# Two causal attentions, a low-rank MLP and a mixture of attention experts on one core: the first two attentions change how they sum, normalise and transpose their rows

## The chip, the cores and the metric

One core of a Trainium2 chip runs the whole program. The metric is the device time of one execution in microseconds (us); the median over several runs is compared. Besides the runs, one execution was taken with the hardware profiler; all durations below come from it.

## The reference

Batch B = 4, H = 12 heads, S = 448 positions, head size 64, model width D = 768, hidden width 3072, rank 32, 4 experts. Cut to what matters:

```python
scores = q @ k.T / 8                       # causal mask
attn = exp(scores - max); attn /= attn.sum(-1) + 1e-9
x = (attn @ v) as (B, S, 768)
h = x.T @ U @ V                            # U 448x32, V 32x448: along the positions
u = x + h.T
x = u + relu(u @ w_ch1) @ w_ch2            # 768 -> 3072 -> 768
...                                        # then top-2 of 4 single-head attention experts on x
```

The change lies in the first three lines of the attention and in the low-rank step, for batch elements 0 and 1.

## The kernel before, in words

Layout. Activations lie with the model width on the 128 partitions and the 448 positions along the free dimension; f32 data that TensorE multiplies in f16 is split into a high and a low half (`hi`, `lo`), and products are made of three passes (hi*hi, hi*lo, lo*hi; `PASS`). All of SBUF is one tensor, `arena`, all of PSUM one tensor, `bank`, of eight banks, so every row of the profile names only these two.

Attention of a batch element b (`attention`, L763) runs over six pairs of heads; pair n is 6 b + p. For each pair:

- `softmax` (L585): for each of two heads f32 score matmuls in four row blocks of 112 (widths 112, 224, 336, 448, because of the causal mask) into the score banks; VectorE adds the mask, finds the row extreme and writes the rows to SBUF (a custom reduction, printed as CUSTOM_DVE_ANT_0 by the profile and as ISA in the order of instructions); ScalarE takes the exponential of each block with the row sum as an accumulated output, then copies each block to f16 (`hi`); GpSimd subtracts to get `lo`; one DMA transpose per head brings hi and lo of the head's ten 112x112 blocks to the layout that the next matmul needs.
- `shares` (L641): from the row sums VectorE forms scaled reciprocals in 112x8 (add and scale, reciprocal, cast to f16, low half); 16 small matmuls spread them over the partitions, and ScalarE copies them to `y`.
- `weighted` (L662): 24 matmuls weight the values (three passes, four blocks, two heads that lie side by side in the array's columns), VectorE multiplies by `y`, ScalarE and GpSimd make f16 halves of the result (`XHL`).
- `lowrank` (L679): a DMA transpose of the halves (`XTR`), 12 f16 matmuls with the three-pass U (`U3`), ScalarE and VectorE bring the sum to f16 halves, one f16 matmul of 448 columns with V, and VectorE adds the result to x (the close of the pair). It is issued for pair n-1 while pair n is under way.

Meanwhile `weight_pair` (L819) decodes the f64 weights of the MLP, finds a power-of-two norm of each tile (four small VectorE steps on 128x2) and writes f16 halves; `mlp` (L898) multiplies. `ORDER` (L47) says which attention, MLP group and expert step follow which.

The order of the instructions. No call issues at once: `Program.add` (L195) records each operation with its engine, cost and key (its due time), and `Program.plan` (L241) makes one fixed list over all engines by keys that the table `SHIFTS` (L51) moves for each part of the program. Where the list leaves TensorE idle before `WARM_END` (210 us of the plan) or in the tail after the last attention, it inserts filler matmuls of zeros of 448 columns (`prog.idle`, L1334). These are instructions like others: on the chip TensorE runs them whether or not it would have had to wait. Every recorded operation has the line of the call in `issue` (L353), so rows are told apart by shape; only fillers have a line of their own.

Of the kernel before, what the change touches and what calls it, by code (L numbers as in the profile page):

```python
# [20 lines left out]
NP = H // 2  # L21
# [58 lines left out]
class Program:  # L80
# [6 lines left out]
    CHAIN = 0.0  # L87
    SLACK = 1.03
# [152 lines left out]
    def plan(self, keys, users):  # L241
# [15 lines left out]
        while len(order) < len(ops):  # L257
# [19 lines left out]
            o = ops[i]  # L277
            cost, fill = o["cost"] * self.SLACK, 0
# [78 lines left out]
def kernel(  # L357
# [96 lines left out]
    XHL = [view("xhl", i * 2048, 128, F16, 1024).rearrange("p (l s) -> p l s", l=2) for i in range(2)]  # L454
# [3 lines left out]
    U3 = view("u3", 0, 128, F16, 2 * NC * 3 * R).rearrange("p (l c r) -> p l c r", l=2, c=NC)  # L458
# [203 lines left out]
    def weighted(vs, pts, y, dst, coef=None, kind="o"):  # L662
        shares(y, coef)
        t = psum(kind)
        with prog.group():
            for i, (lp, lv_) in enumerate(PASS):
                for j in range(NC):
                    for h, (va, pt) in enumerate(zip(vs, pts)):
                        o = t[64 * h:64 * h + 64]
                        k0, kc, kj = LO_BLK if lp else HI_BLK  # L670
                        k = k0 + (kc + kj) * j
                        mm(o[:, C * j:S], va[:, j, 64 * lv_:64 * lv_ + 64],
                           pt[0:C, k:k + kc * (NC - 1 - j) + 1:kc],
                           i == 0 and j == 0, i == 2 and j == NC - 1)
        dve.tensor_tensor(out=y, in0=t[:, 0:S], in1=y, op=ALU.mult)
        act.activation(dst[:, 0, 0:S], y, AF.Copy)
        pool.tensor_tensor(out=dst[:, 1, 0:S], in0=y, in1=dst[:, 0, 0:S], op=ALU.subtract)

    def lowrank(n):  # L679
        b, p = divmod(n, NP)  # L680
        iv = IV[:, b:b + 1]
        tst = TST
        sp.dma_start_transpose(out=XTR, in_=XHL[n % 2].rearrange("p l s -> p (l s)"))
        t = psum("l")
        with prog.group():
            for c in range(NC):
                for i, (lu_, lx) in enumerate(PASS):
                    mm(t[0:96, 0:128], U3[:, lu_, c], XTR[:, 4 * lx + c], c == 0 and i == 0, c == NC - 1 and i == 2)
# [4 lines left out]
        mm(u[:, 0:S], tst, VST, True, True)  # L693
        dve.tensor_tensor_reduce(out=X3[b][:, p], in0=u[:, 0:S], in1=X3[b][:, p], scale=iv, scalar=BIG,
# [68 lines left out]
    def attention(b):  # L763
        if b == B - 1:
            prog.key = HT * 30
            zero_pads(SLOTS[b][1][2:])
        if not b:
# [3 lines left out]
        for p in range(NP):  # L771
# [6 lines left out]
            if p == NP - 1 and b + 1 < B:  # L778
                v_scale(b + 1)
            i = n % 2  # L780
            pts = [SLOTS[b][2][(2 * n + j) % len(SLOTS[b][2])] for j in range(2)]
            prog.key = HT * 2 * n
            softmax([[(QK[i][64 * j:64 * j + 64, 1], QK[i][64 * j:64 * j + 64, 0])] for j in range(2)], -0.125,
                    pts, slots=SLOTS[b][0:2])
            prog.key = HT * (2 * n + 1)
            weighted([VH[:, 2 * i + j] for j in range(2)], pts, X3[b][:, p], XHL[i])
# [32 lines left out]
    def weight_pair(i):  # L819
# [410 lines left out]
    UR = view("ring", 0, 128, I32, 2 * NC * R)  # L1230
    US = view("ring", 2048, 128, F32, NC * R)
    VR = view("ring", 4096, 96, I32, 2 * S)
    LV = view("ring", 8192, 96, F32, S)
# [14 lines left out]
    dve.memset(ONE, 1.0)  # L1248
    prog.key = 0.0
# [7 lines left out]
    for a in XHL:  # L1257
        dve.memset(a[:, :, S:512], 0.0)
# [4 lines left out]
    absmax(TMP[:, 5:6], US)  # L1263
# [16 lines left out]
    for r in range(3):  # L1280
        split(U3V[:, 0, :, r], U3V[:, 1, :, r], USV, SUV[:, 0:1])
# [99 lines left out]
```

## Time and profile before

| | us |
|---|---|
| runs (3): median, lowest, highest | 1050.6, 1049.38, 1054.52 |
| profiled execution: device time | 1048.72 |
| profiled execution: span in the trace | 1045.8 |
| TensorE busy (share of the span) | 1023.3 (98%) |
| VectorE busy | 698.5 (67%) |
| ScalarE busy | 617.8 (59%) |
| GpSimd busy | 466.8 (45%) |
| granted TensorE clock, mean | 0.998 |

The profile covers one execution. PE is TensorE, PEld its weight loads, DVE VectorE, ACT ScalarE, POOL GpSimd, SP the engine that issues all DMAs. Busy times of groups are unions of intervals; successive instructions overlap a little, so groups add up to somewhat more than the engine's total. Share of the span is an average over stages: the first 190 us hold attentions 0 and 1, then come MLP groups, experts and the other attentions.

### The profile page before, as it was taken

Reading aid. Unit: us, or ns where it says so; the run is one execution under the profiler, and the core shown is the slowest. Engines: PE = TensorE matmul, PEld = TensorE weight load, DVE = VectorE, ACT = ScalarE, POOL = GpSimd, SP = SyncE. Lnnn points to the kernel's source line nnn. Section 1 sums busy time; section 2 is a strip of 40 time slices with the busy share of each in tenths; the row PEclk is TensorE's granted clock in tenths of the full one; section 3 lists DMA queues with packets and bytes.
Section 4 is the critical chain, followed back from the end, with each engine's and each line's share of the span. In section 5 each row is a group of like instructions: output and inputs, shape, how many; then the busy total and the mean of one; then the engine's idle time right before and its main releaser. Section 6 shows DMA issues by size and latency. Waiting matters only on the chain.

```text
span 1045.8 us, 18647 instructions
## 1 busy us (share of the span) xinstructions
PE 1023.3 (98%) x6743; PEld 544.7 (52%) x6743; DVE 698.5 (67%) x1744; ACT 617.8 (59%) x1470; POOL 466.8 (45%) x500
## 2 busy tenths in 40 slices
PE   9999989999998999999999999999999999999998
PEld 4555545555544445644555644455555555655555
DVE  8989878878876677555657555588656577531364
ACT  6788987666754563568762569763552632622073
POOL 3576666433552440135540137567797891310011
PEclk9999999999999999999999999999999999999999
DMA  9999999467788786269994269983434345453023
GB/s 240 206 239 240 223 223 266 161 218 249 264 271 286 289 326 218 97 157 232 232 244 128 73 157 219 237 172 104 136 121 151 123 149 156 104 147 106 10 78 107
DMA packets 220139, 192.53 MB, mean 184 GB/s; under 512 B 176304, under 2 KB 179504, under 8 KB 220048
## 3 DMA queue, kind: packets, MB, share of 16 engines
q1 hardware_dynamic: 220048, 191.36, 67.1%
q8 instruction: 52, 0.85, 0.3%
q14 instruction: 39, 0.32, 0.1%
HBM read 112.16 MB, written 36.18 MB: 142 GB/s over the span
## 4 chain that ended last, share of the span: by engine, by line
PE 58%; DMA 6%; DVE 3%; ACT 2%; issue 1%; SPq 0%; DVEq 0%; ACTq 0%
PE bank L353 58%; DVE arena L353 3%; DMA arena<-arena 2%; DMA w<-arena 2%; ACT arena L353 1%; DMA arena<-in_w_dram 1%; PE bank L1334 1%; DMA arena<-in_v_dram 1%; DMA out_dram<-arena 1%; ACT bank L353 0%; SPq L353 0%; DVEq L353 0%; ACTq L353 0%
## 5 line engine op out<-in xcount | busy, mean ns | idle before, releaser
L353 PE MATMUL bank<-arena 128*128 128x448 f16 (+13 forms) x6341 | 945.5, 325 | 17.2 <-ACT arena L353 6.7
L353 POOL TENSOR_TENSOR arena<-arena 128x384 f16<-128x384 f32 (+8 forms) x493 | 465.8, 966 | 568.3 <-ACT arena L353 497.9
L353 PEld LDWEIGHTS <-arena 128*128 128x128 f16 (+5 forms) x5853 | 472.3, 104 | 411.2 <-issue 63.4
L353 ACT ACTIVATE arena<-arena 128x768 f16<-128x768 f32 (+12 forms) x872 | 479.9, 586 | 222.2 <-DVE arena L353 132.7
L353 DVE SCALAR_TENSOR_TENSOR arena<-arena 128x768 int32<-128x768 int32 (+7 forms) x193 | 179.2, 944 | 7.2 <-ACT arena L353 5.8
L353 DVE CUSTOM_DVE_ANT_0 arena<-bank,arena 112x224 f32<-112x224 f32 (+4 forms) x280 | 124.4, 476 | 58.6 <-PE bank L353 51.5
L353 DVE TENSOR_TENSOR arena<-bank,arena 128x448 f16<-128x448 f32 (+2 forms) x160 | 95.5, 599 | 101.4 <-ACT arena L353 75.7
L353 DVE SCALAR_TENSOR_TENSOR arena<-bank,arena 128x448 f32<-128x448 f32 (+1 forms) x138 | 84.6, 621 | 69.9 <-PE bank L353 59.4
L353 DVE TENSOR_SCALAR arena<-arena 128x1 f32<-128x1 f32 (+10 forms) x305 | 85.8, 308 | 46.5 <-ACT arena L353 19.4
L353 ACT ACTIVATE arena<-bank 128x448 f16<-128x448 f32 (+2 forms) x148 | 76.0, 518 | 47.7 <-PE bank L353 44.8
L353 DVE TENSOR_TENSOR arena<-arena 112x8 f16<-112x8 f32 (+10 forms) x136 | 82.4, 618 | 27.6 <-ACT arena L353 25.4
L353 ACT ACTIVATE bank<-bank,arena 128x448 f32<-128x448 f32 x72 | 43.0, 598 | 97.0 <-PE bank L353 96.8
L1334 PE MATMUL bank<-arena 128*128 128x448 f16 x402 | 88.5, 360 | 1.5 <-DVE arena L1251 1.0
L353 ACT ACTIVATE arena<-bank,arena 128x448 f32<-128x448 f32 (+2 forms) x73 | 33.0, 457 | 56.1 <-PE bank L353 53.3
L353 PEld LDWEIGHTS bank<-arena 64*112 64x112 f32 (+5 forms) x488 | 39.4, 169 | 43.1 <-issue 16.7
L353 DVE TENSOR_REDUCE arena<-arena 128x1 f32<-128x448 f32 (+8 forms) x107 | 57.7, 544 | 4.4 <-DMA arena<-in_v_dram 3.3
L1334 PEld LDWEIGHTS <-arena 128*128 128x128 f16 x402 | 37.4, 101 | 42.6 <-issue 12.2
L353 ACT ACTIVATION_READ_ACCUMULATOR arena<-arena 112x1 f32 (+1 forms) x304 | 57.3, 189 | 0.0
L353 DVE DVE_READ_ACCUMULATOR2_ANT arena<- 112x1 f32 (+1 forms) x280 | 22.8, 82 | 0.0
L353 DVE CAST arena<-arena 112x8 f16<-112x8 f32 x32 | 11.7, 372 | 1.7 <-PE bank L353 1.3
L353 DVE TENSOR_SCALAR arena<-bank 128x2 f32<-128x2 f32 x24 | 3.6, 152 | 6.1 <-PE bank L353 6.1
L353 DVE COPY arena<-bank 128x1 f32<-128x1 f32 (+2 forms) x14 | 2.2, 158 | 8.1 <-PE bank L353 8.1
(11 smaller groups left out, 18.8 us busy)
## 6 DMA issues: line engine op xcount, KB each, us to landing
arena<-w SPq DMA_DIRECT2D x138, 384.0 KB, 3.4
arena<-in_w_dram SPq DMA_DIRECT2D x48, 768.0 KB, 5.4
w<-arena SPq DMA_DIRECT2D x78, 384.0 KB, 4.9
arena<-in_qk_dram SPq DMA_DIRECT2D x24, 448.0 KB, 4.3
arena<-in_v_dram SPq DMA_DIRECT2D x24, 224.0 KB, 4.4
out_dram<-arena SPq DMA_DIRECT2D x24, 224.0 KB, 2.2
arena<-in_we_dram SPq DMA_DIRECT2D x6, 384.0 KB, 6.2
arena<-arena SPq DMA_TRANSPOSE x88, 4.9
```

The lines of the kernel that those rows point to most:

```text
L353: fn(*a, **k)
L1334: prog.idle = lambda late: nc.tensor.matmul(bank[:, 0 if late else 7, 64:512], ZERO.to_broadcast([128, 128]), ZERO.to_broadcast([128, S]), ...
```

## The change

For batch elements 0 and 1 `softmax`, `weighted` and `lowrank` are replaced; elements 2 and 3 and the experts keep the old functions.

- `packed`: the scores of both heads lie in one grid of 20 blocks of 112 columns. The exponentials have no accumulated sum. One ScalarE copy makes the f16 high half of all 20 blocks, four GpSimd subtractions of five blocks make the low half; one DMA transpose moves the high halves of both heads, another the low halves.
- `gathered`: row sums are made by 16 matmuls of the transposed halves with a block of ones (`ONE16`), two heads side by side, in the same loop as the 24 value matmuls. ScalarE copies the sums and adds epsilon, VectorE takes the reciprocal of 128x448 and multiplies. Four f32 matmuls with the identity transpose the result, ScalarE copies it out (`XNF`).
- `lowrank32`: four f32 matmuls with U (`UF`), a ScalarE copy, one f32 matmul of 448 columns with V, then the same closing step (`finish`). The DMA transpose of the f16 halves is gone for these pairs.
- `weight_pair`: three of the four norm steps work on the PSUM bank.
- The planner skips, when VectorE or GpSimd would wait more than 100 ns for the shared port, to an operation that needs none (`SKIP`); the table `SHIFTS` has new numbers throughout.

```diff
 SHIFTS = (
-    -77, -44428, 37506, -91735, 18953, 8775, 17019, -24054, -47040, 356689, 6182, -12585, -8654, 13276, -10536,
...
+    -43466, -27356, -10820, 4351, -7110, 8009, -7508, -69, -27832, 14181, 3461, 33477, -8645, -7372, 6786, -6709,
...
+    SKIP = 100.0
...
+            if o["port"] and port > t + self.SKIP:
+                held = []
+                while r and ops[r[0][1]]["port"] and len(held) < 64:
+                    held.append(heapq.heappop(r))
+                if r and len(held) < 64:
+                    j = heapq.heappop(r)[1]
+                    heapq.heappush(r, (keys[i], i))
+                    i, o = j, ops[j]
...
+    def packed(n):
...
+        for j in range(2):
+            for c in range(NC):
+                act.activation(rows(j, c), rows(j, c), AF.Exp, bias=mx[j][:, c:c + 1], scale=-1.0)
+        act.activation(hi[:, :, 0:C], grid, AF.Copy)
+        sp.dma_start_transpose(out=pts[0], in_=HALF[i][0])
+        for k in range(0, 20, 5):
+            pool.tensor_tensor(out=lo[:, k:k + 5, 0:C], in0=grid[:, k:k + 5], in1=hi[:, k:k + 5, 0:C],
+                               op=ALU.subtract)
+        sp.dma_start_transpose(out=pts[1], in_=HALF[i][1])
+        return pts
+
+    def gathered(n, pts):
...
+        den, num, t = psum("b"), psum("o"), psum("l")
+        for l, pt in enumerate(pts):
+            with prog.group():
+                for j in range(NC):
+                    for lv_ in ((None, 0, 1) if not l else (None, 0)):
+                        for h in range(2):
+                            va = ONE16 if lv_ is None else VH[:, 2 * (n % 2) + h, j, 64 * lv_:64 * lv_ + 64]
+                            o = (den if lv_ is None else num)[64 * h:64 * h + 64, C * j:S]
+                            k0, kc = (6 * j, 5) if h else (1 + 6 * j, 1)
+                            mm(o, va, pt[0:C, k0:k0 + kc * (NC - 1 - j) + 1:kc],
+                               not l and j == 0 and lv_ != 1, l == 1 and j == NC - 1)
+        act.activation(y, den[:, 0:S], AF.Identity, bias=EPSC)
+        dve.reciprocal(y, y)
+        dve.tensor_tensor(out=y, in0=num[:, 0:S], in1=y, op=ALU.mult)
+        with prog.group():
+            for c in range(NC):
+                mm(t[0:C, 128 * c:128 * c + 128], y[:, C * c:C * c + C], IDF, True, True)
+        act.activation(XNF[n % 2], t[0:C], AF.Copy)
+
+    def lowrank32(n):
+        b, p = divmod(n, NP)
+        t = psum("l")
+        with prog.group():
+            for c in range(NC):
+                mm(t[0:R, 0:128], UF[:, R * c:R * c + R], XNF[n % 2][:, 128 * c:128 * c + 128], c == 0, c == NC - 1)
+        act.activation(TSF[n % 2], t[0:R, 0:128], AF.Copy)
+        u = psum("l")
+        mm(u[:, 0:S], TSF[n % 2], LV[0:R], True, True)
+        finish(n, u)
...
-        dve.tensor_scalar(s, norm, FLOOR2, None, op0=ALU.max)
-        dve.tensor_scalar(bits(p), bits(s), 1, HALFM, op0=ALU.logical_shift_right, op1=ALU.bitwise_and)
-        dve.tensor_scalar(bits(s), bits(p), HALFM, None, op0=ALU.bitwise_xor)
-        dve.tensor_scalar(s, s, 2.0 ** 57, None, op0=ALU.mult)
+        dve.tensor_scalar(norm, norm, FLOOR2, None, op0=ALU.max)
+        dve.tensor_scalar(bits(p), bits(norm), 1, HALFM, op0=ALU.logical_shift_right, op1=ALU.bitwise_and)
+        dve.tensor_scalar(bits(norm), bits(p), HALFM, None, op0=ALU.bitwise_xor)
+        dve.tensor_scalar(s, norm, 2.0 ** 57, None, op0=ALU.mult)
```

How the instructions stand now. On VectorE, at the first pair's shares in the kernel before (the scale and the reciprocal of 112x8 lie between two score reductions; the cast and the low half follow some ten rows further on):

```order
L353 TENSOR_SCALAR arena<-arena 112x8
L353 ISA arena<-bank,arena 112x112
L353 ISA arena 112x1
L353 RECIPROCAL arena<-arena 112x8
L353 ISA arena<-bank,arena 112x336
L353 ISA arena 112x1
L353 COPY arena<-bank 128x2
L353 TENSOR_REDUCE arena<-bank 1x1
```

and on VectorE at the first pair's reciprocal in the changed kernel:

```order
L363 ISA arena<-bank,arena 112x4x112
L363 ISA arena 112x1
L363 RECIPROCAL arena<-arena 128x448
L363 ISA arena<-bank,arena 112x448
L363 ISA arena 112x1
L363 TENSOR_TENSOR arena<-bank,arena 128x448
L363 TENSOR_REDUCE arena<-arena 112x1 x2
L363 ISA arena<-bank,arena 112x112
```

The reciprocal is now of 448 elements and stands right ahead of a later pair's score reduction and of the product (TENSOR_TENSOR) that the transposes on TensorE need. On TensorE, at the start of the first low-rank group in the kernel before (12 matmuls of 96x128 that needed a DMA transpose; L1334 is the filler):

```order
L1334 LDWEIGHTS arena
L1334 MATMUL bank<-arena 128x448
L353 LDWEIGHTS arena
L353 MATMUL bank<-arena 96x128
L353 LDWEIGHTS arena
L353 MATMUL bank<-arena 96x128
```

and on TensorE at the first transposes of normalised rows in the changed kernel (L1447 is its filler, 112x128 the f32 transposes, 64x448 the next pair's row sums and values):

```order
L1447 LDWEIGHTS arena
L1447 MATMUL bank<-arena 128x448
L363 MATMUL bank<-arena 112x112 x2
L363 MATMUL bank<-arena 112x336 x2
L363 MATMUL bank<-arena 112x128 x4
L363 LDWEIGHTS arena
L363 MATMUL bank<-arena 64x448
```

What waited for a DMA transpose now waits for VectorE's product, with the next pair's row sums and values behind it in the list.

## Rows read from the trace of the kernel before

**Rows 1.** Head of the page: span; busy time, share and instructions of each engine.
```profile
span 1045.8 us, 18647 instructions
PE 1023.3 (98%) x6743; PEld 544.7 (52%) x6743; DVE 698.5 (67%) x1744; ACT 617.8 (59%) x1470; POOL 466.8 (45%) x500
```
**Rows 2.** Busy time by stage of the filler matmuls alone (L1334): PE, PEld.
```profile
0.00:200.00 200.00, 80.36 (x364) 33.78 (x364) 1.00 0.98 230
200.00:1000.00 800.00, 0.00 (x0) 0.00 (x0) 1.00 0.62 178
1000.00:1046.00 46.00, 8.12 (x38) 3.59 (x38) 0.99 0.34 89
```
**Rows 3.** Timeline of VectorE at the close of pair twelve: start, us, what.
```profile
189.10 0.68 DVE L353 CUSTOM_DVE_ANT_0 arena<-bank,arena 128x448 f32<-128x448 f32 x1
```
**Rows 4.** Busy time by stage, all engines; the first row names the columns.
```profile
core 0: us, PE busy (x) PEld busy (x) DVE busy (x) ACT busy (x) POOL busy (x), PEclk, DMA share, GB/s
0.00:190.00 190.00, 183.83 (x1407) 95.68 (x1408) 164.07 (x498) 150.56 (x409) 114.03 (x139) 1.00 1.00 230
```
**Rows 5.** Waits of VectorE, 0 to 190 us: total, times, longest.
```profile
DVE arena L353 <- PE bank L353: 15.9, 16, 3.4
DVE arena L353 <- ACT arena L353: 4.7, 8, 1.2
```
**Rows 6.** Timeline of TensorE, pieces of the first stage: fillers, shares, low rank, values, scores.
```profile
99.36 2.85 PE L1334 MATMUL bank<-arena 128*128 128x448 f16 x14
...
33.34 0.75 PE L353 MATMUL bank<-arena 112*64 112x112 f16 x16
...
109.98 0.83 PE L353 MATMUL bank<-arena 128*96 128x128 f16 x12
...
111.70 1.62 PE L353 MATMUL bank<-arena 112*64 112x448 f16 x24
...
107.30 1.01 PE L353 MATMUL bank<-arena 64*112 64x448 f32 x4
```
**Rows 7.** Groups by shape, weight loads: count, busy us, mean ns, idle before.
```profile
L353 PEld LDWEIGHTS bank<-arena 128*128 128x128 f32 x48 | 8.4, 194 | 11.2 <-ACT arena L353 10.0
```
**Rows 8.** Groups by shape, VectorE, 0 to 190 us.
```profile
L353 DVE CAST arena<-arena 112x8 f16<-112x8 f32 x12 | 7.5, 627 | 0.5 <-PE bank L353 0.5
L353 DVE TENSOR_SCALAR arena<-arena 128x2 int32<-128x2 int32 x13 | 6.5, 500 | 0.1
L353 DVE SCALAR_TENSOR_TENSOR arena<-bank,arena 32x128 f16<-32x128 f32 x12 | 4.1, 343 | 2.8 <-ACT arena L353 2.4
L353 DVE TENSOR_SCALAR arena<-arena 112x8 f32<-112x8 f32 x12 | 4.1, 339 | 1.4 <-ACT arena L353 1.3
L353 DVE TENSOR_TENSOR arena<-arena 112x8 f16<-112x8 f32 x12 | 3.4, 285 | 0.0
L353 DVE RECIPROCAL arena<-arena 112x8 f32<-112x8 f32 x12 | 2.3, 195 | 0.1
```
**Rows 9.** Groups by shape, VectorE: reciprocals from 430 us on, the others whole span.
```profile
L353 DVE RECIPROCAL arena<-arena 112x8 f32<-112x8 f32 x20 | 4.0, 202 | 0.6
L353 DVE RECIPROCAL arena<-arena 112x4 f32<-112x4 f32 x4 | 0.7, 178 | 0.1
...
L353 DVE TENSOR_REDUCE arena<-arena 128x1 f32<-128x448 f32 x48 | 29.3, 612 | 0.6
...
L353 DVE TENSOR_SCALAR arena<-bank 128x2 f32<-128x2 f32 x24 | 3.6, 152 | 6.1 <-PE bank L353 6.1
...
L353 DVE TENSOR_REDUCE arena<-arena 128x1 f32<-128x128 f32 x1 | 0.3, 275 | 0.0
```
**Rows 10.** Groups by shape, ScalarE and GpSimd, 0 to 190 us.
```profile
L353 ACT ACTIVATION_READ_ACCUMULATOR arena<-arena 112x1 f32 x96 | 18.2, 189 | 0.0
...
L353 POOL TENSOR_TENSOR arena<-arena 112x448 f16<-112x448 f32 x24 | 27.9, 1172 | 8.8 <-ACT arena L353 8.6
```
**Rows 11.** Busy time around a wait of TensorE; columns as in rows 4.
```profile
316.30:318.40 2.10, 0.05 (x1) 0.00 (x0) 1.65 (x3) 0.94 (x2) 0.00 (x0) 1.00 1.02 303
318.40:321.80 3.40, 3.37 (x10) 1.62 (x11) 2.15 (x4) 0.00 (x0) 0.00 (x0) 0.50 1.00 408
```

More of the change, by code (lines that the diff above doesn't have):

```diff
@@ L277, in plan @@
             o = ops[i]
+            if o["port"] and port > t + self.SKIP:
[6 more added lines that the diff above has]
+                    i, o = j, ops[j]
+                for x in held:
+                    heapq.heappush(r, x)
             cost, fill = o["cost"] * self.SLACK, 0
@@ L453 @@
     ]
-    XHL = [view("xhl", i * 2048, 128, F16, 1024).rearrange("p (l s) -> p l s", l=2) for i in range(2)]
+    XHL = [view("xhl", i * 2048, 128, F16, 1024).rearrange("p (l c x) -> p l c x", l=2, c=NC) for i in range(2)]
+    XNF = [view("xhl", i * 2048, C, F32, 512) for i in range(2)]
+    GRID = [[view("p", 0, C, F32, 2 * PW), view(r, 10752, C, F32, 2 * PW)] for r in ("x3", "hid")]
+    HALF = [PHL[0:2], SPARE]
+    LV = view("wv", 0, 96, F32, S)
+    UF = view("wv", 1792, C, F32, NC * R)
+    TSF = [view("wv", 2304 + 512 * i, R, F32, 128) for i in range(2)]
+    ONE16 = view("wv", 3328, C, F16, HD)
+    EPSC = view("wv", 3456, 128, F32, 1)
     XTR = view("xtr", 0, 128, F16, 1024).rearrange("p (k e) -> p k e", k=8)
@@ L675, in weighted @@
         dve.tensor_tensor(out=y, in0=t[:, 0:S], in1=y, op=ALU.mult)
-        act.activation(dst[:, 0, 0:S], y, AF.Copy)
-        pool.tensor_tensor(out=dst[:, 1, 0:S], in0=y, in1=dst[:, 0, 0:S], op=ALU.subtract)
+        if len(dst.shape) == 4:
+            hi, lo = [dst[:, l, :, 0:C] for l in range(2)]
+            y = y.rearrange("p (c x) -> p c x", c=NC)
+        else:
+            hi, lo = dst[:, 0, 0:S], dst[:, 1, 0:S]
+        act.activation(hi, y, AF.Copy)
+        pool.tensor_tensor(out=lo, in0=y, in1=hi, op=ALU.subtract)
@@ new lines, in packed, with rows @@
+    def packed(n):
+        b, i = n // NP, n % 2
+        grid, (hi, lo) = GRID[b][i], HALF[i]
+        grid, hi, lo = [a.rearrange("p (k x) -> p k x", x=a.shape[-1] // 20) for a in (grid, hi, lo)]
+        pts = [PT[(2 * n + l) % 3] for l in range(2)]
+        mx = [MX[(2 * n + j) % 4] for j in range(2)]
+        def rows(j, c):
+            return grid[:, 5 * c:6 * c + 1] if j else grid[:, 1 + c:6 * c + 2:5]
+        for cs in ((0, 2), (1,), (3,)):
+            ts = [psum("s") for _ in range(2)]
+            at = {}
+            with prog.group():
+                o = 0
+                for c in cs:
+                    w = C * (c + 1)
+                    for j in range(2):
+                        r = slice(64 * j, 64 * j + 64)
+                        at[j, c] = ts[j][0:C, o:o + w]
+                        mm(at[j, c], QK[i][r, 1, C * c:w], QK[i][r, 0, 0:w], True, True)
+                    o += w
+            for j in range(2):
+                for c in cs:
+                    w = C * (c + 1)
+                    dve.tensor_tensor_reduce(
+                        out=rows(j, c), in0=at[j, c].rearrange("p (k x) -> p k x", x=C),
+                        in1=MASK[:, S - w:S].rearrange("p (k x) -> p k x", x=C), scale=-0.125, scalar=-BIG,
+                        op0=ALU.add, op1=ALU.min, accum_out=mx[j][:, c:c + 1])
+        for j in range(2):
+            for c in range(NC):
[7 more added lines that the diff above has]
+        return pts
@@ new lines, in gathered @@
+    def gathered(n, pts):
+        b, p = divmod(n, NP)
+        y = X3[b][:, p]
+        den, num, t = psum("b"), psum("o"), psum("l")
[16 more added lines that the diff above has]
+        act.activation(XNF[n % 2], t[0:C], AF.Copy)
@@ L679, in lowrank @@
+    def lowrank32(n):
+        b, p = divmod(n, NP)
+        t = psum("l")
+        with prog.group():
+            for c in range(NC):
[4 more added lines that the diff above has]
+        finish(n, u)
     def lowrank(n):
         b, p = divmod(n, NP)
-        iv = IV[:, b:b + 1]
+        if b < 2:
+            lowrank32(n)
+            return
@@ L682, in lowrank @@
         tst = TST
-        sp.dma_start_transpose(out=XTR, in_=XHL[n % 2].rearrange("p l s -> p (l s)"))
+        sp.dma_start_transpose(out=XTR, in_=XHL[n % 2].rearrange("p l c x -> p (l c x)"))
         t = psum("l")
@@ L687, in lowrank @@
                 for i, (lu_, lx) in enumerate(PASS):
-                    mm(t[0:96, 0:128], U3[:, lu_, c], XTR[:, 4 * lx + c], c == 0 and i == 0, c == NC - 1 and i == 2)
+                    mm(t[0:96, 0:128], U3[:, lu_, c], XTR[0:C, 4 * lx + c], c == 0 and i == 0, c == NC - 1 and i == 2)
         act.activation(tst, t[0:96, 0:128], AF.Copy, scale=CT[0:96])
@@ L693, in lowrank, with finish @@
         mm(u[:, 0:S], tst, VST, True, True)
+        finish(n, u)
+    def finish(n, u):
+        b, p = divmod(n, NP)
+        iv = IV[:, b:b + 1]
         dve.tensor_tensor_reduce(out=X3[b][:, p], in0=u[:, 0:S], in1=X3[b][:, p], scale=iv, scalar=BIG,
@@ L766, in attention @@
             zero_pads(SLOTS[b][1][2:])
+        if b == 2:
+            prog.key = HT * 30
+            for a in XHL:
+                dve.memset(a[:, :, :, C:128], 0.0)
         if not b:
@@ L780, in attention @@
             i = n % 2
-            pts = [SLOTS[b][2][(2 * n + j) % len(SLOTS[b][2])] for j in range(2)]
             prog.key = HT * 2 * n
[L783 to L786, printed above, removed]
+            if b < 2:
+                pts = packed(n)
+                prog.key = HT * (2 * n + 1)
+                gathered(n, pts)
+            else:
+                pts = [SLOTS[b][2][(2 * n + j) % len(SLOTS[b][2])] for j in range(2)]
+                softmax([[(QK[i][64 * j:64 * j + 64, 1], QK[i][64 * j:64 * j + 64, 0])] for j in range(2)], -0.125,
+                        pts, slots=SLOTS[b][0:2])
+                prog.key = HT * (2 * n + 1)
+                weighted([VH[:, 2 * i + j] for j in range(2)], pts, X3[b][:, p], XHL[i])
             if p:
@@ L1229 @@
     dve.memset(view("sm", 0, 128, F32, SM), 0.0)
-    UR = view("ring", 0, 128, I32, 2 * NC * R)
-    US = view("ring", 2048, 128, F32, NC * R)
+    UR = view("ring", 0, C, I32, 2 * NC * R)
+    US = UF
     VR = view("ring", 4096, 96, I32, 2 * S)
-    LV = view("ring", 8192, 96, F32, S)
     load_pair(0)
@@ L1248 @@
     dve.memset(ONE, 1.0)
+    dve.memset(ONE16, 1.0)
+    dve.memset(EPSC, EPS)
     prog.key = 0.0
@@ L1256 @@
     prog.key = HT * 0.3
-    for a in XHL:
-        dve.memset(a[:, :, S:512], 0.0)
     zero_pads(PHL[0:2] + SPARE)
@@ L1262 @@
     decode(LV, VR)
-    absmax(TMP[:, 5:6], US)
+    absmax(TMP[0:C, 5:6], US)
     absmax(TMP[0:96, 6:7], LV)
@@ L1280 @@
     for r in range(3):
-        split(U3V[:, 0, :, r], U3V[:, 1, :, r], USV, SUV[:, 0:1])
+        split(U3V[:, 0, :, r], U3V[:, 1, :, r], USV, SUV[0:C, 0:1])
     act.activation(VST, LV, AF.Copy, scale=SUV[0:96, 1:2])
```

4 lines of the change are left out of this document (2 added, 2 removed), and 45 rows, old and new, of the table SHIFTS.

## Prediction

> **What bounds the kernel now.** I read the table of engines first, then the busy time by stage, then the filler matmuls, then what VectorE waited for. TensorE is busy 98% of the span [rows 1], so at first sight every microsecond of its work counts. But part of that work computes nothing: 364 filler matmuls, 80.4 us, stand before 200 us, none between 200 and 1000 us, and 38 near the end [rows 2]. So two stages must be told apart. In the first 190 us (the twelve head pairs of attentions 0 and 1; the last pair's closing VectorE step starts at 189.1 us [rows 3]) TensorE has spare time, and VectorE is the busiest engine that does only useful work: 164.1 us of 190, against 150.6 for ScalarE and 114.0 for GpSimd [rows 4]. Of VectorE's 25.9 idle microseconds there 15.9 were waits for TensorE [rows 5]. From 190 us on there are nearly no fillers and TensorE is itself the bound. What the change is worth is therefore decided by when the first stage ends: the fillers removed say what was planned, and VectorE says whether that can be had.
>
> **The change on TensorE.** The sum is made against the profiled execution, 1048.7 us (a span of 1045.8 [rows 1] and 2.9 around it), which is 1.9 us under the median of the three runs; differences carry over to the median. TensorE's instructions are listed in a fixed order, fillers included, so a filler that is not issued is time saved unless the engine waits there instead. The new order has 211 fillers where 402 stood; 173 are left ahead of the end of attention 1, where 364 were, and 38 at the end as before. Fourteen of them took 2.85 us [rows 6], so 0.20 each: 191 x 0.20 = 38.2 us less.
>
> Against that stands new work in each of twelve pairs. Removed are the 16 small matmuls that spread the shares (0.75 us), the 12 of the f16 low rank (0.83 us) [rows 6] and one f16 matmul of 448 columns (0.20, as a filler): 1.78 us. Added are 16 row-sum matmuls in the form of the 24 that weight the values; those took 1.62 us [rows 6], so two thirds, 1.08 us. Added too are eight f32 matmuls of 128 columns and one of 448. Their nearest row is the f32 score of 448 columns, 1.01 us for two heads that share the array [rows 6]. Alone, one lies between half of that and all of it: 0.50 to 1.01; I take 0.90, since each streams its own columns through half of the rows at the same time as the other. For 128 columns the same gives 0.14 to 0.29; I take 0.24, and as the upper end 0.39, two f32 weight loads of 0.194 us [rows 7], should the loads not hide. Sum per pair: 1.08 + 8 x 0.24 + 0.90 - 1.78 = 2.12 us, twelve times 25.4 us (ends 11 and 41). TensorE alone: -38.2 + 25.4 = **-12.8 us** (ends -27 and +3).
>
> **The change on VectorE.** Gone before 190 us are four groups of operations on 112x8 (the scale, reciprocal, cast and low half of the shares) and the low half of the f16 low-rank step, twelve each: 7.5 + 4.1 + 3.4 + 2.3 + 4.1 = 21.4 us [rows 8]. The 128x2 integer steps of the weight norm move from SBUF to PSUM: 13 of 0.500 us [rows 8] become steps of 0.152 as the one on PSUM now takes [rows 9], 4.5 us less. Added is one thing whose price decides: twelve reciprocals of 128x448. The trace has them on 8 and on 4 elements only. On 8 they took 202 ns and on 4 178 ns [rows 9]: 6.0 ns for each further element, and so 0.202 + 440 x 0.0060 = 2.84 us. Simple operations don't behave so: a reduction of 448 took 612 ns where 128 took 275 [rows 9], 1.05 ns per element. With that slope a reciprocal would be 0.66 us, the lower end. The upper end, eight times 1.05 ns per element, is 3.77 us. I take 2.84, the reciprocal's own slope. Twelve make 34.1 us. GpSimd has four subtractions per pair instead of eight and no f16 low half of the result to make; a cast of 112x8 took 627 ns where the reciprocal of the same size took 195 [rows 8], which I read as waiting beside GpSimd's traffic; for fewer such waits in the operations that stay I take 3 us off (ends 0 and 6). VectorE's load up to the close of pair twelve becomes 164.1 - 21.4 - 4.5 + 34.1 - 3 = **169.3 us**.
>
> The Trainium skill weighs this both ways. "VectorE: DVE Perf Modes", section "First, the fixed hardware budget", says that the reciprocal runs an iterative divide with a repeat count of 8, which speaks against this change; the row agrees that an element is dear, though 6.0 ns lies below eight steps of the reduction's slope. The same page's cycle table (section on SBUF-source operations) gives one element per cycle to an ordinary f32 operation, by which the sum would end at TensorE's -12.8 us; the two reciprocal rows speak against it.
>
> **Both together.** If TensorE never waited, its part of pair twelve would close at 189.1 - 38.2 + 25.4 - 2.8 (by the orders 14 fewer MLP matmuls stand ahead of it, to be done later) = 173.5 us. VectorE has 169.3 us of work until there, so its idle time would have to fall from 25.9 to 4.2 us. Neither end is likely: part of the idle time is the start and hand-over of banks (each set of scores fills both score banks, and the next waits until VectorE has read them), part is waiting for scores that stand behind fillers, and that part shrinks. I take half, 13 us: VectorE closes pair twelve at 182.3 us, and TensorE, whose transposes of the normalised rows wait for VectorE's product, stands 8.8 us longer than planned. -12.8 + 8.8 = **-4 us**: 1044.7 in the profiled execution, 1046.6 against the median.
>
> What else moves costs nothing here. ScalarE loses the 96 accumulator reads of the exponentials, 18.2 us before 190 us, and most of the fixed cost of eight copies; GpSimd's 1.17 us subtractions of 448 [rows 10] become 560-element ones, half as many. Both were less loaded than VectorE [rows 4], so their relief is covered by it, and so are the twelve shorter transposes that leave SP's queue: they take latency out of a pair, not work from VectorE. Were that cover gone, with ScalarE the bound, the first stage could not shrink to less than its present 150.6 us less 18.2. Behind the long reciprocal stands, on VectorE, the next pair's score reduction; its bank comes free 2.2 us later than with a cheap one, and TensorE's next scores are late next. After 420 us the work is the same in both; a new order may shift it by a few microseconds either way.
>
> **The rivals.** First, **the reciprocals are hidden**: VectorE's idle time shrinks to the 4 us, or the divide is cheap after all, and TensorE sets the end: -12.8 us, 1037.8. For it speaks that 15.9 of the idle microseconds were waits for TensorE; against it the two reciprocal rows and the short margin. Second, slower, **eight steps per element**: at 3.77 us the twelve reciprocals add 11.2 us to VectorE, TensorE stands 20 us at the transposes, and the sum is +7.2: 1057.8. It decides from 3.2 us per reciprocal on, where the whole saving on TensorE is eaten. For it: the steep slope; against it: the slope is measured at 6.0, not 8.4 ns. The repeat count on the Trainium skill's page "VectorE: DVE Perf Modes" (section "First, the fixed hardware budget") names this case. Third, **the waits drop TensorE's clock**: after 2.1 us without matmuls the granted clock was 0.50 (1.2 of 2.4 GHz) for 3.4 us [rows 11], 1.7 us lost. The fillers were what kept such gaps out of this stage; if half of the twelve new waits reach 2 us, six such drops cost 10 us: 1056.6. Against it, 8.8 us over twelve pairs is 0.7 us each.
>
> **How the numbers follow.** Forecast 0.38, hidden 0.28, eight steps 0.14, clock 0.10, something else in the new order 0.10. A measurement of this kernel can tell about 0.5%, 5.3 us, from no change. The forecast's own range is -9 to +3 us (idle time of 8 to 20 us), mostly within that bound with a quarter of it beyond on the fast side. Faster: nearly all of hidden, that quarter and a third of the rest, 0.38. Slower: nearly all of eight steps, most of clock, a third of the rest, 0.25. Same: 0.37. With the first rival's TensorE price (down to 1036) and all idle time kept (+8.9 us, 1059.5) or clock drops on top, the range is 1036 to 1062; the likeliest time is 1047.
>
> **What would show it.** Right: 211 fillers; reciprocals of 128x448 near 2.8 us; VectorE busier than 92% until the close of pair twelve, which comes at 180 to 185 us; TensorE idle for VectorE some 9 us more than before in that stage; groups of four f32 transposes near 1 us. Wrong: reciprocals under 1 us or over 3.5; the close of pair twelve near 174 us; waits for ScalarE or a transfer in that stage; or a difference that arises after 420 us.

## The result, and the profile after

The changed kernel took 1063.9 us (median of 4 runs, 1060.2 to 1067.8) where the kernel before took 1050.6 beside it: a ratio of 1.0121 [1.0084, 1.0158], 13 us slower. The forecast was 1047, its range ended at 1062. The profiled execution took 1060.2 us, with a span of 1058.5; it answers to the 1045.8 of [rows 1]. It is the fastest of the four: the others took 1.4, 6.0 and 7.6 us longer at mean granted clocks of 0.994, 0.989 and 0.992 against its 0.995, so some of the median's 3.7 us more may be the clock's, which no trace here can show.

The head of its page:

```profile
span 1058.5 us, 18104 instructions
PE 1022.1 (97%) x6612; PEld 546.9 (52%) x6612; DVE 717.8 (68%) x1698; ACT 601.3 (57%) x1290; POOL 441.4 (42%) x440
```

The filler matmuls alone (L1447; PE, PEld), to be read beside [rows 2]:

```profile
0.00:200.00 200.00, 41.54 (x173) 16.00 (x173) 0.98 0.84 208
```

The timeline of VectorE at the close of pair twelve, which stood at 189.1 us in [rows 3]:

```profile
198.76 0.68 DVE L363 CUSTOM_DVE_ANT_0 arena<-bank,arena 128x448 f32<-128x448 f32 x1 [0.41 <-PE bank L363]
```

Busy time by stage, cut at that close (columns as in [rows 4]), with two stretches in which the clock was down:

```profile
0.00:198.80 198.80, 178.40 (x1253) 95.62 (x1254) 180.41 (x450) 135.86 (x231) 91.99 (x79) 0.98 0.84 207
198.80:1058.50 859.70, 843.68 (x5360) 451.31 (x5358) 537.36 (x1249) 465.41 (x1059) 349.40 (x363) 1.00 0.60 172
69.80:73.20 3.40, 3.40 (x26) 2.00 (x22) 1.24 (x2) 0.32 (x1) 0.23 (x1) 0.50 0.24 67
93.70:97.10 3.40, 2.77 (x9) 1.05 (x10) 3.40 (x14) 2.19 (x3) 1.85 (x2) 0.50 0.70 159
```

So the span grew by 12.7 us, 9.7 of them before the close of pair twelve. What follows the close takes 859.7 us instead of 856.7 (1045.8 - 189.1), about the 2.8 us of MLP matmuls that the prediction had deferred to there. The first stage is the whole question. VectorE has 180.4 us of work in it, 91%, and TensorE now waits. The waits up to the close (who waited for whom: total, times, longest), to be read beside [rows 5]; the last line is TensorE's wait for VectorE in the kernel before:

```profile
PE bank L363 <- DVE arena L363: 19.4, 14, 3.5
DVE arena L363 <- PE bank L363: 9.1, 12, 2.6
DVE arena L363 <- ACT arena L363: 3.6, 4, 1.8
...
PE bank L353 <- DVE arena L353: 0.3, 1, 0.3
```

Groups by shape up to the close, VectorE first; the reciprocal answers to [rows 9], the f32 matmuls are the new transposes, the sum with U, the product with V, and the narrowest scores (the profile has two records for each f32 matmul of the program):

```profile
L363 DVE RECIPROCAL arena<-arena 128x448 f32<-128x448 f32 x12 | 35.3, 2944 | 0.8 <-ACT arena L363 0.8
L363 DVE SCALAR_TENSOR_TENSOR arena<-arena 128x768 int32<-128x768 int32 x26 | 33.1, 1276 | 0.1
...
L363 PE MATMUL bank<-arena 128*112 128x128 f32 x96 | 13.3, 282 | 10.9 <-DVE arena L363 10.9
L363 PE MATMUL bank<-arena 112*32 112x128 f32 x96 | 12.7, 276 | 0.7 <-DVE arena L363 0.7
L363 PE MATMUL bank<-arena 32*128 32x448 f32 x24 | 12.2, 586 | 0.0
...
L363 PE MATMUL bank<-arena 64*112 64x112 f32 x48 | 6.8, 314 | 2.8 <-DVE arena L363 2.8
```

Of TensorE's 19.4 us of waiting for VectorE 10.9 stand ahead of the transposes. The other 8.5 are spread over the stage; 3.8 of them stand ahead of scores (2.8 in the row above, 1.0 ahead of those of 224 columns), whose bank VectorE has to read first.

The reciprocals and the decode of the MLP weights (128x768) make over a third of VectorE's time. The decode was not a term of the prediction; in the kernel before, by the same view (0 to 190 us), it read:

```profile
L353 DVE SCALAR_TENSOR_TENSOR arena<-arena 128x768 int32<-128x768 int32 x25 | 26.3, 1054 | 0.1
```

The chain of waits that ended at the close shows how the two engines are tied; first its shares of the 198.8 us, then its pieces from 61.67 to 85.95 us (start, us, what; the first drop of the clock lies in the piece at 68.39):

```profile
by line: DVE arena L363 41.4%; PE bank L363 34.5%; PE bank L1447 9.7%; issue 8.0%; ACT arena L363 4.8%; POOL arena L363 0.6%; ACT bank L363 0.5%; DVE bank L363 0.2%; DVE arena L1366 0.0%; DVEq L363 0.0%; ACTq L363 0.0%
...
61.67 6.59 DVE arena L363 x11
68.25 0.14 issue
68.39 6.17 PE bank L363 x38
74.56 0.03 issue
74.59 5.16 DVE arena L363 x7
79.75 0.04 issue
79.79 5.40 PE bank L363 x43
85.19 0.76 PE bank L1447 x4
```

Neither engine bounds the stage by itself. VectorE makes the product, TensorE transposes it and goes on to scores, VectorE reduces the scores: 41% of the chain is VectorE, 44% TensorE (fillers included). The chain passes from one to the other, and in the stage each is idle for some 20 us (18.4 and 20.4).

### The profile page after: what moved, and what is told of

Its sections match the earlier page's. It is cut to its first block, busy times and chain, and to the rows that moved or that the text cites. A ratio compares the mean times of both kernels' runs of the same rounds, so it can differ in the third digit from the quotient of the medians.

```text
span 1058.5 us, 18104 instructions
## 1 busy us (share of the span) xinstructions
PE 1022.1 (97%) x6612; PEld 546.9 (52%) x6612; DVE 717.8 (68%) x1698; ACT 601.3 (57%) x1290; POOL 441.4 (42%) x440
## 4 chain that ended last, share of the span: by engine, by line
PE 67%; DVE 12%; DMA 8%; issue 6%; ACT 4%; POOL 2%; SPq 0%; DVEq 0%; POOLq 0%; ACTq 0%
PE bank L363 65%; DVE arena L363 12%; DMA arena<-in_w_dram 5%; ACT arena L363 4%; PE bank L1447 3%; POOL arena L363 2%; DMA w<-arena 1%; DMA arena<-arena 1%; DMA out_dram<-arena 1%; ACT bank L363 0%; SPq L363 0%; DVE bank L363 0%; DVEq L363 0%; POOLq L363 0%; DVE arena L1366 0%
## 5 line engine op out<-in xcount | busy, mean ns | idle before, releaser
L363 PE MATMUL bank<-arena 128*128 128x448 f16 (+16 forms) x6401 | 978.2, 330 | 31.8 <-DVE arena L363 24.0
L363 POOL TENSOR_TENSOR arena<-arena 128x384 f16<-128x384 f32 (+8 forms) x433 | 440.4, 1040 | 606.5 <-ACT arena L363 470.0
L363 PEld LDWEIGHTS <-arena 128*128 128x128 f16 (+3 forms) x5697 | 466.9, 104 | 407.1 <-issue 67.0
L363 ACT ACTIVATE arena<-arena 128x448 f16<-128x448 f32 (+15 forms) x776 | 459.4, 629 | 229.4 <-DVE arena L363 131.4
L363 ACT ACTIVATE arena<-bank 128x448 f16<-128x448 f32 (+4 forms) x160 | 79.9, 503 | 59.6 <-PE bank L363 58.7
L363 PEld LDWEIGHTS bank<-arena 64*112 64x112 f32 (+7 forms) x704 | 64.3, 164 | 73.8 <-issue 34.6
L363 DVE TENSOR_TENSOR arena<-arena 128x448 f16<-128x448 f32 (+9 forms) x124 | 84.5, 694 | 26.0 <-ACT arena L363 24.4
L363 DVE TENSOR_SCALAR arena<-arena 128x1 f32<-128x1 f32 (+11 forms) x221 | 69.5, 340 | 45.3 <-DMA arena<-in_w_dram 14.8
L1447 PE MATMUL bank<-arena 128*128 128x448 f16 x211 | 49.7, 371 | 1.0 <-DVE arena L1366 1.0
L363 DVE RECIPROCAL arena<-arena 112x8 f32<-112x8 f32 (+2 forms) x36 | 40.1, 1113 | 1.4 <-ACT arena L363 0.8
L1447 PEld LDWEIGHTS <-arena 128*128 128x128 f16 x211 | 19.6, 103 | 26.6 <-issue 12.4
```

Source lines behind the costliest of these rows:

```text
L363: fn(*a, **k)
L1447: prog.idle = lambda late: nc.tensor.matmul(bank[:, 0 if late else 7, 64:512], ZERO.to_broadcast([128, 128]), ZERO.to_broadcast([128, S]), ...
```

## The experiments

Theory: the long reciprocals lengthen the first stage through VectorE, whose idle time can't be had back. Rivals: the new order itself, the f32 work on TensorE, and the clock drops. The first stage of all kernels, from the busy time cut at the close of pair twelve of each profile (us; idle is close less VectorE), with the median time of the runs; the kernel before took 1051.4 to 1051.7 us beside runs 1 to 9, and each ratio is to that. Runs 4 and 5 were planned anew: 56 more and 34 fewer MLP matmuls lie ahead of their closes than in the changed kernel.

| kernel | close | VectorE | its idle | TensorE | time |
|---|---|---|---|---|---|
| before | 189.1 | 163.2 | 25.9 | 182.9 | 1050.6 |
| changed | 198.8 | 180.4 | 18.4 | 178.4 | 1063.9 |
| 1 cheap step for the reciprocal | 173.0 | 151.5 | 21.5 | 170.9 | 1036.6 |
| 2 every second one cheap | 185.6 | 161.6 | 24.0 | 173.9 | 1051.5 |
| 3 before, reciprocals added | 216.0 | 191.4 | 24.6 | 194.5 | 1075.0 |
| 4 planned at the measured cost | 220.9 | 190.4 | 30.5 | 215.2 | 1084.4 |
| 5 shares as before, rest changed | 181.3 | 152.9 | 28.4 | 174.5 | 1047.7 |
| 6 fillers in the waits | 205.4 | 180.3 | 25.1 | 191.1 | 1068.5 |
| 7 short GpSimd steps | 195.1 | 169.8 | 25.3 | 177.9 | 1058.7 |
| 8 exp(-ln x) on ScalarE | 173.9 | 143.3 | 30.6 | 171.6 | 1035.1 |
| 9 as 8, half of the fillers | 177.8 | 144.2 | 33.6 | 164.5 | 1038.6 |

**1. A cheap step in the reciprocal's place.** All else, the order too, as in the changed kernel.

```diff
         dve.reciprocal(y, y)
+        prog.ops[-1]["calls"] = [(nc.vector.tensor_scalar, (y, y, 2.0 ** -18, None), dict(op0=ALU.mult))]
```

> The changed kernel, every instruction in the same place, but the twelve reciprocals of 128x448 are replaced by a multiplication with a constant (the rows are then not normalised: that part of the computation is left out). Theory VectorE: the reciprocals' 2.94 us make VectorE the bound of the first stage; without them TensorE's 19.4 us of waiting for VectorE fall under 5, the close of pair twelve comes near 176 us, and the time is 1036 to 1046 us. Rival TensorE: the f32 matmuls and the missing fillers (a lower clock) cost the time by themselves; the time stays above 1055 us.

Measured: 1036.6 us, 0.9854 [0.9795, 0.9912] of the kernel before. The step took 0.62 us, 2.33 less than a reciprocal; VectorE's load fell by 28.9 us, and the close came 25.8 us earlier. TensorE's waits for VectorE, busy time up to the close, and the shares of the chain that ended there:

```profile
PE bank L363 <- DVE arena L363: 0.6, 2, 0.4
...
0.00:173.00 173.00, 170.93 (x1253) 93.75 (x1254) 151.50 (x450) 134.92 (x231) 92.21 (x79) 1.00 1.00 239
...
by line: PE bank L363 62.6%; PE bank L1448 18.1%; DVE arena L363 6.7%; DMA arena<-in_w_dram 4.1%; DMA arena<-arena 3.1%; POOL arena L363 2.4%; ACT arena L363 1.5%; issue 0.8%; ACT bank L363 0.3%; DVE arena L1367 0.0%; DVEq L363 0.0%
```

TensorE is busy for 99% of the stage and 81% of the chain. The order and the f32 work are cleared: with them the kernel is faster than before. The reciprocal's length is what costs.

**2. Every second reciprocal cheap.** As 1, with `if n % 2:` ahead of the new line.

> The changed kernel, same order, with every second of the twelve reciprocals of 128x448 replaced by a multiplication with a constant (half of the pairs are then not normalised: that part of the computation is left out). Theory VectorE: the wait grows with the load from the first reciprocal on, because VectorE's idle time of some 20 us can't be used: half of the loss, 1046 to 1054 us, close of pair twelve 183 to 189 us. Rival threshold: VectorE's idle time takes in six reciprocals (14 us): under 1042 us.

Measured: 1051.5 us, 0.9990 [0.9962, 1.0017]. Busy time up to the close:

```profile
0.00:185.60 185.60, 173.93 (x1253) 93.88 (x1254) 161.64 (x450) 135.38 (x231) 91.87 (x79) 0.99 0.88 223
```

Six dear reciprocals move the close by 12.6 us (173.0 to 185.6), the other six by 13.2: about 2.15 us each, 92% of the 2.33 that each is longer. There is no point up to which they are free. VectorE's load rose by 10.1 and by 18.8 us in these two steps, because the steps beside the reciprocals took more or less long; the close followed the reciprocals' own length and not the load.

**3. The kernel before, with twelve such reciprocals added** ahead of the product with `y`, into a spare buffer.

```diff
+            prog.ops[-1]["calls"].insert(0, (nc.vector.reciprocal, (view("wv", 0, 128, F32, S), y), {}))
```

> The kernel before, same order, with one more reciprocal of 128x448 on VectorE in each of the twelve pairs of attentions 0 and 1, right ahead of the product, into memory that nothing reads then. Theory VectorE: its load of 163 us until the close of pair twelve becomes 198, and with some 12 us of idle time the close comes near 210 us: 1066 to 1078 us. Rival TensorE: VectorE has 26 idle us there and takes most of it in; under 1058 us.

Measured: 1075.0 us, 1.022 [1.017, 1.027]. Busy time up to the close, one of six stretches of the first 160 us with the clock at 0.50 or near it, and what TensorE waited for longest:

```profile
0.00:216.00 216.00, 194.54 (x1402) 99.60 (x1403) 191.35 (x508) 151.76 (x409) 110.35 (x138) 0.94 0.87 202
48.70:55.50 6.80, 6.51 (x30) 2.51 (x30) 3.80 (x11) 3.89 (x12) 2.23 (x4) 0.50 0.65 188
...
PE bank L353 <- DVE arena L353: 17.9, 11, 2.9
```

Twelve of 2.946 us, 35.4 in all, raise VectorE's load by 28.2 and move the close by 26.9. The price, 2.24 us each, is much the same in an order that knows nothing of the change. Here the clock is part of it: TensorE's busy time grew by 11.6 us with the same number of matmuls.

**4. The measured cost in the planner.** Its cost of a reciprocal becomes 2950 ns; the table stays, the order and the fillers (386 instead of 211) come out anew.

```diff
+            if method == "reciprocal" and m > 16:
+                return 2950.0, 88.0
```

> The changed kernel, but its planner is told that the reciprocal of 128x448 costs 2.95 us, not 0.53; same table of shifts. 386 fillers instead of 211. Theory VectorE: VectorE's load is the same, fillers only take the place of waits: the close of pair twelve not before 194 us, 1058 to 1070 us. Rival order: the reciprocals cost because the order was made for cheap ones; planned with their price most of the loss comes back, 1053 us or less.

Measured: 1084.4 us, 1.0315 [1.0264, 1.0367]: above what either of the two expected. TensorE's waits for VectorE are all but gone:

```profile
PE bank L365 <- DVE arena L365: 2.1, 4, 0.9
```

The stage grew by 22.1 us all the same. The 175 fillers more (34.6 us) fill TensorE's list (215.2 of 220.9 us), and of VectorE's 30.5 us of idle time 16.1 are waits for TensorE. Part of the growth is other work, though: 36 decode steps instead of 26 and 216 MLP matmuls instead of 160 lie ahead of this close, and yet what follows it takes 865.9 us instead of 859.7, for a reason that wasn't looked for. That the order was planned at a wrong cost is therefore not what made the change slow, with this table at least; no new table was searched.

**5. Shares as before, the rest of the change kept.** The exponentials accumulate their sums again, `shares` makes `y` from reciprocals of 112x8, and the row-sum matmuls and the long reciprocal are gone.

```diff
+        shares(y, which=n % 2)
...
-        act.activation(y, den[:, 0:S], AF.Identity, bias=EPSC)
-        dve.reciprocal(y, y)
```

> The changed kernel without its row sums by TensorE: sums from the accumulated exponentials and shares of 112x8 spread by 16 small matmuls as before, all else as changed (one grid, f32 transposes, f32 low rank), planned with the changed table. Theory VectorE: twelve reciprocals of 2.94 us go and about 17 us of small steps come back, so VectorE has some 18 us less to do before the close of pair twelve, which comes at 176 to 184 us: 1040 to 1050 us. Rival TensorE: the f32 part is what costs; above 1055 us.

Measured: 1047.7 us, 0.9966 [0.9929, 1.0003]: all but the reciprocal is worth a small gain at most, in an order that wasn't tuned for it. VectorE's load is 27.5 us lower than in the changed kernel, where 18 were expected; 7.6 of that is the decode, beside the same 48 subtractions of GpSimd:

```profile
L363 DVE SCALAR_TENSOR_TENSOR arena<-arena 128x768 int32<-128x768 int32 x26 | 25.5, 979 | 0.0
...
L363 POOL TENSOR_TENSOR arena<-arena 112x560 f16<-112x560 f32 x48 | 63.7, 1359 | 80.8 <-issue 57.3 <-ACT arena L363 23.5
```

The clock lay at 0.50 for 13.7 us here, the longest drop of all kernels in the first stage. Busy time ahead of it and in it:

```profile
136.00:140.00 4.00, 3.48 (x41) 1.58 (x39) 4.00 (x12) 4.00 (x17) 0.00 (x0) 1.00 1.23 220
140.00:141.70 1.70, 1.26 (x6) 0.58 (x8) 1.70 (x3) 1.70 (x7) 0.00 (x0) 1.00 1.49 112
141.70:155.40 13.70, 12.54 (x55) 7.48 (x52) 7.94 (x22) 9.09 (x18) 7.09 (x6) 0.50 1.06 280
```

**6. Six more fillers ahead of each group of transposes**, where TensorE waits (72 in all).

```diff
+        prog.ops[-1]["calls"][0:0] = [(lambda: prog.idle(False), (), {})] * 6
```

> The changed kernel with six more filler matmuls (1.1 us) on TensorE right ahead of each of the twelve groups of f32 transposes, where it waits for VectorE's product. Theory VectorE: the fillers run inside the waits; the close of pair twelve stays within 3 us of 198.8 us and the time within 5 us of 1064, whether the clock drops or not. Rival clock: the two drops of the clock in the first stage are what the waits cost; they go, and the time falls by 3 us or more.

Measured: 1068.5 us, 1.0170 [1.0141, 1.0199], 4.6 us above the changed kernel: the time is at the very edge of what the theory allowed, and the close, at 205.4 us, is 6.6 later and not within 3. The waits for VectorE, and busy time up to the close:

```profile
PE bank L363 <- DVE arena L363: 11.7, 10, 2.7
...
0.00:205.40 205.40, 191.10 (x1325) 102.95 (x1326) 180.34 (x450) 136.17 (x231) 90.78 (x79) 0.98 0.84 201
```

TensorE has 12.7 us more of work and waits 7.7 less, and the close moves by 6.6. VectorE's load is the same to 0.1 us; its idle time went from 18.4 to 25.1. The wait ahead of the transposes fell from 10.9 to 1.2 us, but the one ahead of the narrowest scores rose from 2.8 to 5.5. So work put into TensorE's waits is half free only: VectorE's load is not a bound that absorbs the rest. The clock fell in two stretches here too, so this run can't say what the drops cost.

**7. Short GpSimd steps.** In the timeline of the changed kernel one decode step took 4.08 us, beside six subtractions of GpSimd that ran from 55.16 to 62.52 us; steps that met no GpSimd instruction took 0.95, as the one at 82.69 (VectorE, then GpSimd; start, us, what):

```profile
57.67 4.08 DVE L363 SCALAR_TENSOR_TENSOR arena<-arena 128x768 int32<-128x768 int32 x1
...
82.69 0.95 DVE L363 SCALAR_TENSOR_TENSOR arena<-arena 128x768 int32<-128x768 int32 x1
...
55.16 7.36 POOL L363 TENSOR_TENSOR arena<-arena 112x560 f16<-112x560 f32 x6
```

The run cuts the subtractions of ten of the twelve pairs to a seventh:

```diff
+            if n > 1:
+                prog.ops[-1]["calls"] = [(nc.gpsimd.tensor_tensor, (), dict(out=lo[:, k:k + 5, 0:16], in0=grid[:, k:k + 5, 0:16],
+                                       in1=hi[:, k:k + 5, 0:16], op=ALU.subtract))]
```

> The changed kernel in its own order, with the GpSimd subtractions of pairs three to twelve cut from 560 to 80 elements each (the low halves of the attention rows are left out for the rest). In the changed kernel a decode step of 128x768 took 0.95 us where it met no GpSimd instruction and up to 4.08 us where it did, 1.276 on average. Theory of the port (VectorE's steps wait out GpSimd's instructions, and that is the part of its load that was missed): the decode steps fall to 0.95 to 1.05 us on average, VectorE's load up to the close of pair twelve falls from 180.4 to 170 to 174, that close comes at 187 to 194 us instead of 198.8, and the time is 1051 to 1059 us. Rival (the hand-overs between VectorE and TensorE set the end whatever VectorE's load is): the decode steps shorten as well, but the load that is saved comes back as idle time, the close stays above 196 us and the time above 1060 us.

Measured: 1058.7 us, 1.0064 [1.0041, 1.0086]; the profile is of an execution of 1061.4. The decode and the stage:

```profile
L363 DVE SCALAR_TENSOR_TENSOR arena<-arena 128x768 int32<-128x768 int32 x26 | 26.3, 1015 | 0.1
...
0.00:195.10 195.10, 177.93 (x1253) 95.35 (x1254) 169.82 (x450) 135.28 (x231) 50.08 (x78) 0.98 0.86 211
```

The median lies at the edge of what the theory of the port expected, the close (195.1) between theory and rival. Both hold in part: VectorE's load fell by 10.6 us, 6.8 of them in the decode, so GpSimd's traffic was what lengthened its steps, but 6.9 us of that came back as idle time. A microsecond taken off these steps moved the close by 0.35 (3.7 of 10.6), one taken off the reciprocals in runs 1 and 2 by 0.92.

**8. 1/x as exp(-ln x) on ScalarE**, in the same order: two steps in place of the copy of the sums, none on VectorE. One load of a table that holds both functions (`natural_log_exp`) stands at the start.

```diff
         act.activation(y, den[:, 0:S], AF.Identity, bias=EPSC)
+        prog.ops[-1]["calls"] = [(nc.scalar.activation, (y, den[:, 0:S], AF.Ln), dict(bias=EPSC)),
+                                  (nc.scalar.activation, (y, y, AF.Exp), dict(scale=-1.0))]
         dve.reciprocal(y, y)
+        prog.ops[-1]["calls"] = []
```

> The changed kernel, every other instruction in the same place, but the reciprocal is made by ScalarE: instead of one copy of the row sums two activations, the logarithm and the exponential of its negative, with one activation table for both; VectorE's reciprocal is gone. Theory VectorE: VectorE loses 35 us before the close of pair twelve; ScalarE gains about 12 x 0.65 = 8 us and has idle time for it; TensorE sets the end as with the cheap stand-in: close near 174 us, 1034 to 1044 us. Rival: the reciprocal's path is a latency in each pair, and two activations lengthen it again: above 1050 us.

Measured: 1035.1 us (1034.1 to 1037.5), 0.9854 [0.9828, 0.9879]: faster than both kernels. ScalarE's two steps and its table load, and busy time by stage:

```profile
L363 ACT ACTIVATE arena<-bank,arena 128x448 f32<-128x448 f32 x12 | 7.5, 625 | 5.0 <-PE bank L363 4.9
...
L363 ACT ACTIVATE arena<-arena 128x448 f32<-128x448 f32 x12 | 6.9, 577 | 0.4
...
L1370 ACT ACT_TABLE_LOAD x1 | 1.3, 1283 | 0.8 <-PEq L1483 0.8
...
0.00:173.90 173.90, 171.59 (x1253) 94.16 (x1254) 143.30 (x437) 140.31 (x243) 90.93 (x79) 1.00 0.98 238
```

The logarithm costs what the copy cost, 0.625 us, and the second step adds 6.9 us to an engine with 33 us to spare, for 35.3 us taken off VectorE.

**9. As 8, with half of the fillers** (78 instead of 173 ahead of the close).

```diff
-            for _ in range(fill):
+            for _ in range(fill if late else fill // 2):
```

> The variant with 1/x as exp(-ln x) on ScalarE, with 78 fillers ahead of the close of pair twelve instead of 173 (95 fewer, 19 us at 0.20 each), all else in the same order. In the variant with all fillers the chain up to that close, 173.9 us, was 84% TensorE and VectorE had 143 us of work. If TensorE's list alone set the end: close at 155 us, time 1016. Theory that some 18 to 26 us of VectorE's idle time can't be had in any order of this kernel: close at 161 to 169 us, time 1023 to 1030 us. Rival clock (the gaps that fillers kept closed drop the granted clock to 0.5 in several stretches of the stage): close above 170 us, time 1032 us or more, granted clock of the stage below 0.95.

Measured: 1038.6 us (1034.6 to 1043.4), 0.9861 [0.9834, 0.9889]; the profile is of an execution of 1043.4. Its stage came out longer than that of 8 (177.8 us), neither the 155 nor the 161 to 169 of two of the theories. Around the one clock drop of the stage:

```profile
42.00:45.90 3.90, 2.90 (x19) 1.78 (x18) 2.99 (x14) 3.64 (x8) 1.78 (x2) 1.00 1.32 212
45.90:56.10 10.20, 8.24 (x40) 4.53 (x39) 6.00 (x16) 4.31 (x6) 5.57 (x4) 0.54 1.01 253
...
PE bank L363 <- DMA arena<-arena: 4.1, 2, 3.0
```

A wait of 3.0 us for a transposing transfer stands in that stretch. The drop can have cost some 4 us (8.24 us of matmuls at half speed), and the clock of the whole stage is 0.97, not under 0.95 as the rival had it, so the drop alone is not the answer. TensorE's idle time grew from 2.3 us in run 8 to 13.3, and its matmuls other than fillers took 143.2 us instead of 131.1; those two, the drop's 4 us among them, ate more than the 19.3 us of fillers. What made the matmuls longer beyond the drop isn't settled.

## Why the prediction was wrong, step by step

- **Where the stage is bound: right in place, too simple in kind.** VectorE did decide, and TensorE stood 10.9 us at the transposes for VectorE's product, where the prediction had 8.8. But I set the close as VectorE's work plus half of its former idle time, and TensorE's other 8.5 us of waits for VectorE I had put at nothing: that the score banks come free later stands under "What else moves costs nothing here", and 3.8 us were waited there.
- **TensorE alone: right in sum, with luck.** 211 fillers, 173 of them ahead of the close. The f32 work measured 38.2 us in twelve pairs, 3.18 each, where 8 x 0.24 + 0.90 = 2.82 was taken. Without waits the close was to come at 173.5 us: runs 1 and 8 have it at 173.0 and 173.9. But TensorE's work there was 170.9 and 171.6 us, where the sum leaves 167.3 (182.9 - 38.2 + 25.4 - 2.8); its idle time, 6.2 us before, shrank to 2.1 and 2.3 and made up for that. The first rival's time, 1037.8, is within 3 us of both.
- **The reciprocal: right.** Its own slope on 4 and 8 elements [rows 9] gave 2.84 us; 2.944 was measured, 6.2 ns for each further element (2944 - 202 over 440). The repeat count of 8 that the Trainium skill gives ("VectorE: DVE Perf Modes", section "First, the fixed hardware budget") agrees with the row in that the divide is dear; eight of the reduction's steps would be 8.4 ns, which the row does not bear out.
- **VectorE's load: failed, 169.3 foretold, 180.4 measured.** Without the reciprocals 145.1 us were left where the working has 135.2. The step that failed is "for fewer such waits in the operations that stay I take 3 us off (ends 0 and 6)": the sign was wrong. The decode alone went from 25 x 1.054 to 26 x 1.276 us, +6.8, which with those 3 us is nearly all of the 9.9. I had reckoned GpSimd's traffic by its total, which did fall (114.0 us [rows 4] to 92.0). Run 7 shows that the subtractions are the cause: with these cut the load is 169.8. Neither their total nor their length foretells it, though: run 5 has the same 48, and its decode took 0.979 us. What counts is which steps meet which subtractions, nine decode steps of 26 here, and that falls out of the timing.
- **VectorE's idle time: failed, and it weighs more.** "I take half, 13 us": 18.4 was measured. Counted so, 11.1 of the 16.5 us by which the close came late are load and 5.4 idle time. But run 7 has the load that I foretold, and its close still came at 195.1 us, not 182.3, with 25.3 us idle: nearly the whole of the former 25.9, as in the far end of the prediction's range (169.3 + 25.9 = 195.2). In none of the eleven profiles is it under 18.4 us. The waits for TensorE in it did shrink in the changed kernel, from 15.9 [rows 5] to 9.1 us, only not by the 13 us that I took. Its length follows from both engines, which take turns in the chain; that reading fits runs 2, 6 and 7 and is not shown step by step.
- **The rivals.** The second one came near in its number and not in its mechanism: TensorE waited 19.4 us for VectorE (the rival said 20 at the transposes, where it was 10.9), and not because an element takes eight steps. Its 1057.8 was still 6 us short. The clock rival is a lesser part in the profiled execution: two drops of 3.4 us at 0.50, 6.17 us of matmuls in them (3.40 + 2.77), which at full speed would have taken half, so at most some 3 us of the 9.7. The drops come with the reciprocals: none in the stage in run 1, one in run 2, two in the changed kernel.
- **After the close: right**, 3.0 us more against 2.8 foretold.

Of the 25.3 us of idle time in run 7 14.6 were waits for TensorE and 4.8 for ScalarE; how much each hand-over makes was not taken apart.

## What to carry to other kernels

Before a new elementwise reciprocal goes onto a busy engine, price it by the slope between two sizes that the trace has, and ask whether an idle engine can make it in another form: here exp(-ln x) on ScalarE turned 13 us lost into some 15 us won, in an unchanged order. Where two engines hand work back and forth in fixed lists, don't count the fuller engine's idle time as available; a step that the other engine waits for costs nearly its whole length when it is lengthened (here 0.92 of it), a step beside that path less (0.35 in run 7). GpSimd's total said nothing of what VectorE lost to it here: look at which steps meet its instructions, and expect that to change with every change of the order or of a step's length.

## What was not expected of the hardware

- VectorE's decode of 128x768 took 0.95 us where it met no GpSimd instruction; of the 26 before the close eight took 1.25 to 2.00 us and one 4.08, all beside GpSimd's subtractions.
- The granted clock fell for 13.7 us in run 5 though no wait of TensorE in the 7 us ahead of it was over 0.7 us: in the 5.7 us before the drop it was busy for 4.74 (3.48 + 1.26). In the kernel before, a stretch with 0.05 us of matmuls in 2.1 cost only 3.4 us at the lower level [rows 11].
